# One level of Strassen in the second MoE product of a fused attention and MoE kernel

## The chip, the cores and the metric

The kernel runs on one core of a Trainium2 chip. The time is the device time of one execution in microseconds (us), as the median of several executions. The span in a profile is shorter than the time of the same execution (before: 435.7 and 437.55), so spans are compared only with spans. TensorE is called PE below (PEld is its loading of weights), VectorE DVE, ScalarE ACT and GpSimd POOL, as in the profile.

## The reference

Attention over 8 batches of 12 heads, 448 tokens and head size 64, with normalised q and k; its output goes through a two-layer MLP with a leaky ReLU. Cut to what matters:

```python
def _attn_ref(q, k, v, g_q, g_k):
    q_n, k_n = (rmsnorm(q, g_q), rmsnorm(k, g_k))
    scores = scale * np.matmul(q_n, k_n.transpose(0, 1, 3, 2))
    scores = scores - np.max(scores, axis=-1, keepdims=True)
    attn = np.exp(scores)
    attn = attn / (np.sum(attn, axis=-1, keepdims=True) + 1e-09)
    return np.matmul(attn, v)

def _moe_ref(x, w_in, w_out):          # x 3584 x 768, w_in 768 x 2048, w_out 2048 x 768
    h = x @ w_in
    g = np.maximum(0.01 * h, h)
    return g @ w_out
```

## The kernel before

Attention is worked in 24 units, three per batch. Each unit has four parts (d = 0 to 3). PE alternates between the scores of the unit and pieces of the MoE products, which come from a queue: `fill` takes pieces of it after each part, and weaves jobs for the other engines between them. The second product of the MoE takes tiles of 128 tokens; gt holds the activations of two batches, with the 2048 hidden features as 16 blocks on the partitions:

```python
    gt = cst.tile([P, FT, 2 * S], FP16)                 # FT = 16, S = 448
    ...
    def moe2(pair, t, half, part):                      # half: 384 of the 768 output columns
        ...
        for ft in range(8 * part, 8 * part + 8):
            nc.tensor.matmul(op2[:, 0:HC], gt[:, ft, ts(t, P)], wout16[:, ft, ds(HC * half, HC)],
                             start=(ft == 0), stop=(ft == FT - 1))
        if part == 0:
            return
        ...
            nc.vector.tensor_copy(ost[0][:, ds(HC * half, HC)], op2[:, 0:HC])
```

The exponentials of a new unit need a shift, which is made from the maximum of its first scores (DVE), spread over the partitions by a small matmul of `dg` (PE), and reduced again (DVE):

```python
                    qk(u, STEPS[d])                     # first scores of the new unit
                    if d == 0:
                        shift_max(u)                    # DVE: maximum of the scores, then dg
                        if narrow(u - 1):
                            pv_slot(u - 1)              # PE: 28 matmuls of the old unit
                            zcol(u - 1)                 # PE: 16 matmuls
                            shift_mm(u)                 # PE: the matmul of dg
                            ...
                    ex(u)                               # ACT: exponentials
```

On DVE the maximum stands behind whatever the last part of the old unit put there: the two normalisations `n` of a later unit, copies of finished output. On POOL run `xt` (x times 1/z), `rq` or `qg` (q times g) and some squares.

## Time and profile before

| | before |
|---|---|
| time, median (lowest to highest) | 436.96 us (436.82 to 437.01, 3 runs) |
| span of the profiled run | 435.7 us |
| busy: PE, DVE, ACT, POOL | 419.9, 215.6, 309.9, 148.8 us |
| mean granted clock of PE | 0.995 |

The row of PE's granted clock has one digit for each fortieth of the span, in tenths of full speed:

```profile
PEclk9899999999999999999999999999999999999999
```

After the second slice, which lies in the start, the digit never falls. The list of waits gives the waiting engine and line, the releaser, the total in us, the number and the longest:

```profile
PE sT L179 <- ACT et L198: 3.8, 9, 0.9
PE pb L228 <- DVE dg L218: 1.8, 3, 0.8
```

The second line is the matmul of dg; only one of its three waits, of 0.84 us, lies after the start. PE is all but free of waits.

### The profile page before, as it was taken

Reading aid. Unit: us, or ns where it says so; the run is one execution under the profiler, and the core shown is the slowest. Engines: PE = TensorE matmul, PEld = TensorE weight load, DVE = VectorE, ACT = ScalarE, POOL = GpSimd, SP = SyncE. Lnnn points to the kernel's source line nnn. Section 1 sums busy time; section 2 is a strip of 40 time slices with the busy share of each in tenths; the row PEclk is TensorE's granted clock in tenths of the full one; section 3 lists DMA queues with packets and bytes.
Section 4 is the critical chain, followed back from the end, with each engine's and each line's share of the span. In section 5 each row is a group of like instructions: output and inputs, shape, how many; then the busy total and the mean of one; then the engine's idle time right before and its main releaser. Section 6 shows DMA issues by size and latency. Waiting matters only on the chain.

```text
span 435.7 us, 8818 instructions
## 1 busy us (share of the span) xinstructions
PE 419.9 (96%) x3714; PEld 216.9 (50%) x3714; DVE 215.6 (49%) x321; ACT 309.9 (71%) x460; POOL 148.8 (34%) x102
## 2 busy tenths in 40 slices
PE   6878999999999999999999999999999999999995
PEld 6645444444455544554445544554445544555563
DVE  4897565874535744554455745555356611220021
ACT  5989878688976699867876699867877486634300
POOL 4997565633422432532430423522521110100000
PEclk9899999999999999999999999999999999999999
DMA  7999995789458856669447875778524530311022
GB/s 262 248 259 255 238 235 76 195 195 201 96 144 145 215 152 119 136 200 201 91 126 141 200 186 98 154 205 165 125 45 100 132 84 2 78 38 38 0 73 73
DMA packets 66315, 62.37 MB, mean 143 GB/s; under 512 B 35684, under 2 KB 61284, under 8 KB 66276
## 3 DMA queue, kind: packets, MB, share of 16 engines
q1 hardware_dynamic: 55840, 49.82, 44.7%
q0 software_dynamic: 10272, 11.80, 17.4%
q8 instruction: 29, 0.48, 0.4%
q10 hardware_dynamic: 164, 0.20, 0.1%
q14 instruction: 10, 0.08, 0.1%
HBM read 45.61 MB, written 11.01 MB: 130 GB/s over the span
## 4 chain that ended last, share of the span: by engine, by line
PE 84%; ACT 7%; DVE 6%; DMA 2%; issue 1%; SPq 0%; DVEq 0%; ACTq 0%
PE hps L329 33%; PE op L351 31%; PE sT L179 8%; PE sT L314 5%; ACT et L198 3%; PE zc L260 3%; DVE n L151 1%; DMA rk<-in_k_dram 1%; PE pb L228 1%; DVE ssq L139 1%; PE sT L243 1%; PE pv L314 1%; ACT et L196 1%; DVE xt L323 1%; DMA out_dram<-ost 1%
## 5 line engine op out<-in xcount | busy, mean ns | idle before, releaser
L198 ACT ACTIVATE et<-sT,eb 128x896 f16<-128x896 f32 x166 | 158.7, 1004 | 48.0 <-PE sT L179 35.7
L351 PE MATMUL op<-wout,gt 128*128 128x384 f16 x896 | 153.6, 326 | 0.0
L329 PE MATMUL hps<-xt,win 128*128 128x448 f16 x756 | 151.0, 353 | 0.2 <-DVE xt L323 0.2
L351 PEld LDWEIGHTS <-gt 128*128 128x128 f16 x896 | 84.7, 98 | 65.3 <-issue 12.2
L329 PEld LDWEIGHTS <-win 128*128 128x128 f16 x756 | 70.9, 98 | 71.8 <-issue 7.6
L294 POOL TENSOR_TENSOR xt<-x,rz 128x896 f16<-128x896 f32 x19 | 40.9, 2154 | 185.6 <-DMA rz<-zs 170.7
L331 ACT ACTIVATE gt<-hps 128x448 f16<-128x448 f32 x126 | 67.6, 543 | 22.6 <-PE hps L329 21.5
L359 DVE COPY ost<-op 128x384 f32<-128x384 f32 x54 | 30.0, 556 | 94.2 <-PE op L351 90.9
L134 POOL TENSOR_TENSOR qg<-rq,ggb 128x896 f32<-128x896 f32 (+2 forms) x25 | 61.3, 2454 | 36.9 <-DVE n L151 32.6
L179 PE MATMUL sT<-qkT 64*64 64x448 f16 x664 | 52.3, 364 | 4.5 <-ACT et L198 3.8
L151 DVE TENSOR_TENSOR n<-qg,rinv 128x896 f16<-128x896 f32 (+2 forms) x25 | 27.1, 1085 | 54.5 <-POOL xt L294 23.6
L139 DVE TENSOR_REDUCE ssq<-sq 128x14 f32<-128x896 f32 (+2 forms) x49 | 50.0, 1054 | 1.9 <-ACT sq L126 1.9
L216 DVE TENSOR_REDUCE sT<-sT 128x1 f32<-128x896 f32 x22 | 24.1, 1094 | 30.6 <-PE sT L179 30.4
L151 DVE TENSOR_TENSOR n<-rk,rinv 128x896 f16<-128x896 f32 (+2 forms) x25 | 34.2, 1372 | 0.0
L179 PEld LDWEIGHTS <-qkT 64*64 64x64 f16 x672 | 15.2, 104 | 37.9 <-issue 35.4
L272 ACT COPY x<-sT 128x896 f32<-128x896 f32 x19 | 17.2, 905 | 18.0 <-PE sT L314 18.0
L314 PE MATMUL sT<-et,vt 64*64 64x448 f16 x532 | 28.4, 349 | 0.0
L314 PEld LDWEIGHTS <-vt 64*64 64x64 f16 x672 | 19.8, 107 | 10.5
L106 POOL DMA_DIRECT2D vt<-in_v_dram x24 | 18.3, 763 | 0.0
L126 ACT ACTIVATE sq<-rq 128x896 f32<-128x896 f32 (+2 forms) x19 | 17.3, 913 | 1.2 <-DMA rq<-in_q_dram 1.2
L126 ACT ACTIVATE sq<-rk 128x896 f32<-128x896 f32 x17 | 16.2, 955 | 0.7 <-DMA rk<-in_k_dram 0.7
L260 PE MATMUL zc<-et,onesr 128*32 128x448 f16 (+1 forms) x304 | 16.1, 332 | 0.0
(66 smaller groups left out, 216.3 us busy)
## 6 DMA issues: line engine op xcount, KB each, us to landing
rq<-in_q_dram SPq DMA_DIRECT2D x24, 448.0 KB, 4.6
rk<-in_k_dram SPq DMA_DIRECT2D x24, 448.0 KB, 6.1
out_dram<-ost SPq DMA_DIRECT2D x54, 192.0 KB, 3.5
rz<-zs SPq DMA_DIRECT2D x38, 224.0 KB, 3.5
vt<-in_v_dram POOLq DMA_DIRECT2D x24, 224.0 KB, 4.7
win<-in_moe_w_in_dram POOLq DMA_DIRECT2D x8, 384.0 KB, 11.5
wout<-in_moe_w_out_dram POOLq DMA_DIRECT2D x2, 1536.0 KB, 26.9
qkT<-n SPq DMA_TRANSPOSE x18, 4.1
```

The lines of the kernel that those rows point to most:

```text
L126: nc.scalar.activation(buf(u, "sq")[:, ti, :, c[0]:c[1]], raw[u][ti][:, :, c[0]:c[1]], AF.Square)
L134: eng.tensor_tensor(buf(u, "qg")[:, :, c[0]:c[1]], raw[u][0][:, :, c[0]:c[1]], ggb[:, None, None, :].broadcast_to([P, 2, n, D]), op=ALU.mult)
L139: nc.vector.tensor_reduce(buf(u, "ssq")[:, ti, :, c[0]:c[1]], buf(u, "sq")[:, ti, :, c[0]:c[1]], axis=AXL.X, op=ALU.add)
L151: nc.vector.tensor_tensor(buf(u, "n16")[:, ti, c[0]:c[1]].rearrange("p s a d -> p a s d"), src[:, :, c[0]:c[1]], buf(u, "rinv")[:, ti, :, ...
L179: nc.tensor.matmul(banks[a][64 * r:64 * r + 64, 0:S].rearrange("p (t x) -> p t x", t=NS), kT(u, r, a, t), qT(u, r, a), start=True, stop=True)
L198: nc.scalar.activation(s["et"][:, t], sT[:, :, 0:S], AF.Exp, bias=s["eb"], scale=1.0)
L294: nc.gpsimd.tensor_tensor(xts[b][:, g], s["x32"], s["rz"], op=ALU.mult)
L314: nc.tensor.matmul(s["pv"][r][64 * a:64 * a + 64, 0:S], vts[u % NV][64 * r:64 * r + 64, a, t], s["et"][64 * r:64 * r + 64, t, a], start=(t ...
L329: nc.tensor.matmul(hps[:, 0:S], win16[:, kt // 2, kt % 2, ts(ft, P)], xt[:, kt // 2, kt % 2], start=(kt == 0), stop=(kt == KT - 1))
L331: nc.scalar.activation(gt[:, ft, ds(S * (b % 2), S)], hps[:, 0:S], AF.Prelu, bias=0.0, scale=1.0, alpha=0.01)
L351: nc.tensor.matmul(op2[:, 0:HC], gt[:, ft, ts(t, P)], wout16[:, ft, ds(HC * half, HC)], start=(ft == 0), stop=(ft == FT - 1))
L359: nc.vector.tensor_copy(ost[0][:, ds(HC * half, HC)], op2[:, 0:HC])
```

## The change

The intent is to take an eighth off the matmuls of each pair of token tiles in the second product; 11 pairs use it, which takes away 88 of the 896 matmuls. For two token tiles A = (a11 a12; a21 a22), split by halves of the hidden features, and the weights B split into four blocks, a product by blocks takes 8 half products of 8 matmuls each. Strassen's scheme, in the form with four sums on either side (s1 to s4 of the activations, four of the weights), takes 7. The sums of the weights are made once. Three of the seven half products are accumulated in PSUM onto others, and the rest is added on DVE on the way out. To make room in SBUF, gt shrinks to one batch and a carry of 64 columns, q times g is written in place, and some pools lose a buffer; the matmul of dg becomes two of 64 columns in spare columns of another bank. The core of the diff:

```diff
-    NV = 5
+    NV = 4
...
-    gt = cst.tile([P, FT, 2 * S], FP16)
+    gt = cst.tile([P, FT, 8 * 64], FP16)
+    tw = cst.tile([P, 4, HF, HC], FP16)          # sums of weights; HF = 8, HC = 384
+    sa = cst.tile([P, 4, HF, P], FP16)           # sums of activations
...
+        if u > 0 and "pslot" in st[u - 1]:       # in shift_mm: dg in two
+            pb = st[u - 1]["pslot"][:, :, S:S + 64]
+            for x in range(2):
+                nc.tensor.matmul(pb[:, x], onesp, s["dg"][:, 64 * x:64 * x + 64], start=True, stop=True)
...
+    def weight_sum(n, x):
+        x = slice(4 * x, 4 * x + 4)
+        a, b = ((wblock(0, 1), wblock(0, 0)), (wblock(1, 1), tw[:, 0]),
+                (wblock(1, 1), wblock(0, 1)), (wblock(1, 0), tw[:, 1]))[n]
+        nc.vector.tensor_tensor(tw[:, n, x], a[:, x], b[:, x], op=ALU.subtract)
+    def s1(tt, x=slice(0, 8)):
+        nc.vector.tensor_tensor(sa[:, 0, x], gblock(tt[1], 0)[:, x], gblock(tt[1], 1)[:, x], op=ALU.add)
+    def s2(tt, x=slice(0, 8)):
+        nc.vector.tensor_tensor(sa[:, 1, x], sa[:, 0, x], gblock(tt[0], 0)[:, x], op=ALU.subtract)
+    ...                                          # s3 = a11 - a21, s4 = a12 - s2, on nc.gpsimd
+    def seven(pair, tt, nxt=None, last=False):   # i0 to i6, each 8 matmuls; "later": at the next piece
+        i0: mm(bank("ma"), gblock(tt[0], 0), wblock(0, 0), True)    # later: DVE copies ma
+        i1: mm(bank("mb"), sa[:, 1], tw[:, 1], True)                # later: DVE adds mb
+        i2: mm(g["ma"], gblock(tt[0], 1), wblock(1, 0), False)      # later: ACT copies ma
+        i3: mm(bank("mc"), sa[:, 0], tw[:, 0], True)                # later: DVE adds mc, s1 of the next pair
+        i4: mm(bank("md"), sa[:, 2], tw[:, 2], True)                # later: DVE adds md
+        i5: mm(g["mc"], sa[:, 3], wblock(1, 1), False)              # later: s2, DVE adds mc, s3, s4
+        i6: mm(g["md"], gblock(tt[1], 1), tw[:, 3], False)          # later: DVE adds md
...
+                if d == 3 and u in (5, 6):
+                    for n in (0, 2) if u == 5 else (1, 3):
+                        for x in range(2):
+                            job(weight_sum, n, x)
```

(The lines i0 to i6 are shortened here from small functions to one line each.)

More of the change, by code (lines that the diff above doesn't have):

```diff
@@ L47 @@
     prep_p = ctx.enter_context(tc.tile_pool(name="prep", bufs=2))
-    small = ctx.enter_context(tc.tile_pool(name="small", bufs=3))
+    small = ctx.enter_context(tc.tile_pool(name="small", bufs=2))
     epool = ctx.enter_context(tc.tile_pool(name="epool", bufs=2))
-    zpool = ctx.enter_context(tc.tile_pool(name="zpool", bufs=2))
+    zpool = ctx.enter_context(tc.tile_pool(name="zpool", bufs=1))
     xpool = ctx.enter_context(tc.tile_pool(name="xpool", bufs=2))
-    opool = ctx.enter_context(tc.tile_pool(name="opool", bufs=3))
+    opool = ctx.enter_context(tc.tile_pool(name="opool", bufs=4))
     psum = ctx.enter_context(tc.tile_pool(name="psum", bufs=1, space=bass.MemoryType.PSUM))
@@ L77 @@
     wout16 = cst.tile([P, FT, DM], FP16)
-    gt = cst.tile([P, FT, 2 * S], FP16)
+    gt = cst.tile([P, FT, 8 * 64], FP16)
+    HF = FT // 2
+    HC = DM // 2
+    tw = cst.tile([P, 4, HF, HC], FP16)
+    sa = cst.tile([P, 4, HF, P], FP16)
     win_v = moe_w_in.rearrange("(g a r d) n -> a d g r n", a=2, r=2, d=D)
@@ L111 @@
     SHAPES = dict(
-        sq=([P, 2, 2, NS, D], FP32, 2), ssq=([P, 2, 2, NS], FP32, 2), uu=([P, 2, 2, NS], FP32, 2),
-        rinv=([P, 2, 2, NS], FP32, 2), qg=([P, 2, NS, D], FP32, 1),
-        n16=([P, 2, NS, 2, D], FP16, 2), qkT=([P, 2, NS, P], FP16, 3))
+        sq0=([P, 2, NS, D], FP32, 3), sq1=([P, 2, NS, D], FP32, 3), ssq=([P, 2, 2, NS], FP32, 2), uu=([P, 2, 2, NS], FP32, 2),
+        rinv=([P, 2, 2, NS], FP32, 2),
+        n16=([P, 2, NS, 2, D], FP16, 1), qkT=([P, 2, NS, P], FP16, 3))
     def buf(u, name):
@@ L118, in buf @@
             shape, dtype, bufs = SHAPES[name]
-            st[u][name] = prep_p.tile(shape, dtype, tag=name, bufs=bufs, name=name)
+            st[u][name] = prep_p.tile(shape, dtype, tag=name[:2] if bufs == 3 and name != "qkT" else name, bufs=bufs, name=name)
         return st[u][name]
@@ L125, in prep_sq @@
         for ti in tis:
-            nc.scalar.activation(buf(u, "sq")[:, ti, :, c[0]:c[1]], raw[u][ti][:, :, c[0]:c[1]], AF.Square)
+            nc.scalar.activation(buf(u, f"sq{ti}")[:, :, c[0]:c[1]], raw[u][ti][:, :, c[0]:c[1]], AF.Square)
     def prep_sqp(u, tis=BOTH):
         for ti in tis:
-            nc.gpsimd.tensor_tensor(buf(u, "sq")[:, ti], raw[u][ti], raw[u][ti], op=ALU.mult)
+            nc.gpsimd.tensor_tensor(buf(u, f"sq{ti}"), raw[u][ti], raw[u][ti], op=ALU.mult)
     def prep_qg(u, eng, c=ALL):
         n = c[1] - c[0]
-        eng.tensor_tensor(buf(u, "qg")[:, :, c[0]:c[1]], raw[u][0][:, :, c[0]:c[1]],
+        eng.tensor_tensor(raw[u][0][:, :, c[0]:c[1]], raw[u][0][:, :, c[0]:c[1]],
                           ggb[:, None, None, :].broadcast_to([P, 2, n, D]), op=ALU.mult)
@@ L138, in prep_ssq @@
         for ti in tis:
-            nc.vector.tensor_reduce(buf(u, "ssq")[:, ti, :, c[0]:c[1]], buf(u, "sq")[:, ti, :, c[0]:c[1]],
+            nc.vector.tensor_reduce(buf(u, "ssq")[:, ti, :, c[0]:c[1]], buf(u, f"sq{ti}")[:, :, c[0]:c[1]],
                                     axis=AXL.X, op=ALU.add)
@@ L149, in prep_norm @@
         for ti in tis:
-            src = (buf(u, "qg"), raw[u][1])[ti]
+            src = raw[u][ti]
             nc.vector.tensor_tensor(
@@ L224, in shift_mm @@
         s = st[u]
-        if "pb" not in s:
-            shift_bank(u)
-        pb = s["pb"]
-        nc.tensor.matmul(pb[:, 0:P], onesp, s["dg"], start=True, stop=True)
-        nc.vector.tensor_reduce(s["spare"][:, 510:511], pb[:, 0:P], axis=AXL.X, op=ALU.max)
+        if u > 0 and "pslot" in st[u - 1]:
+            pb = st[u - 1]["pslot"][:, :, S:S + 64]
+            for x in range(2):
+                nc.tensor.matmul(pb[:, x], onesp, s["dg"][:, 64 * x:64 * x + 64], start=True, stop=True)
+            nc.vector.tensor_reduce(s["spare"][:, 510:511], pb, axis=AXL.XY, op=ALU.max)
+        else:
+            if "pb" not in s:
+                shift_bank(u)
+            pb = s["pb"]
+            nc.tensor.matmul(pb[:, 0:P], onesp, s["dg"], start=True, stop=True)
+            nc.vector.tensor_reduce(s["spare"][:, 510:511], pb[:, 0:P], axis=AXL.X, op=ALU.max)
         s["eb"] = small.tile([P, 1], FP32, tag="eb", name="eb")
@@ L323, in xmul, with prelu @@
             nc.vector.tensor_tensor(xts[b][:, g, r], s["pv"][r][:, 0:S], s["rz"][:, r], op=ALU.mult)
+    def prelu(b, dst, src):
+        if b % 2 == 0:
+            src = src.rearrange("p (t x) -> p t x", t=NS)[:, ::-1]
+            dst = dst.rearrange("p (t x) -> p t x", t=NS)
+        nc.scalar.activation(dst, src, AF.Prelu, bias=0.0, scale=1.0, alpha=0.01)
     def moe1(b, ft):
@@ L330, in moe1 @@
                              start=(kt == 0), stop=(kt == KT - 1))
-        nc.scalar.activation(gt[:, ft, ds(S * (b % 2), S)], hps[:, 0:S], AF.Prelu,
-                             bias=0.0, scale=1.0, alpha=0.01)
+        prelu(b, gt[:, ft, 64 * (b % 2):64 * (b % 2) + S], hps[:, 0:S])
     def moe1_part(b, banks, k0, k1):
@@ L338, in moe1_part, with col, store, flush @@
                                  start=(kt == 0), stop=(kt == KT - 1))
-    ost = {}
+    def col(t):
+        return 64 * (5 - 2 * t) if t < 3 else P * (t - 3)
+    def store(pair, t, tile_, c, last):
+        for y in range(2):
+            n = 2 * t + (1 - y if t < 3 else y)
+            b, grp = 2 * pair + n // NS, n % NS
+            dst = out[b * S:(b + 1) * S, :].rearrange("(p t) m -> p t m", t=NS)
+            eng = nc.scalar if last and y else nc.sync
+            eng.dma_start(dst[:, grp, c], tile_[64 * y:64 * y + 64, c])
+    ost = {}
+    pend = []
+    L, R, LR = slice(0, HC), slice(HC, DM), slice(0, DM)
+    def flush():
+        while pend:
+            pend.pop(0)()
+    def out_tile():
+        return opool.tile([P, DM], FP32, tag="ost", name="ost")
     def moe2(pair, t, half, part):
-        last = pair == B // 2 - 1 and t == NS - 1
+        flush()
         if half == 0 and part == 0:
-            ost[0] = opool.tile([P, DM], FP32, tag="ost", name="ost")
+            ost[0] = out_tile()
         if part == 0:
@@ L348, in moe2 @@
         op2 = ost[1]
-        HC = DM // 2
         for ft in range(8 * part, 8 * part + 8):
-            nc.tensor.matmul(op2[:, 0:HC], gt[:, ft, ts(t, P)], wout16[:, ft, ds(HC * half, HC)],
+            nc.tensor.matmul(op2[:, 0:HC], gt[:, ft, ds(col(t), P)], wout16[:, ft, ds(HC * half, HC)],
                              start=(ft == 0), stop=(ft == FT - 1))
@@ L354, in moe2 @@
             return
-        if last:
-            nc.vector.tensor_copy(ost[0][:, HC * half:HC * half + HC // 2], op2[:, 0:HC // 2])
-            nc.scalar.copy(ost[0][:, HC * half + HC // 2:HC * half + HC], op2[:, HC // 2:HC])
-        else:
-            nc.vector.tensor_copy(ost[0][:, ds(HC * half, HC)], op2[:, 0:HC])
-        if half == 1 or last:
-            c = slice(HC * half, HC * half + HC) if last else slice(0, DM)
-            for y in range(2):
-                bb, grp = divmod(2 * t + y, NS)
-                b = 2 * pair + bb
-                dst = out[b * S:(b + 1) * S, :].rearrange("(p t) m -> p t m", t=NS)
-                eng = nc.scalar if last and y else nc.sync
-                eng.dma_start(dst[:, grp, c], ost[0][64 * y:64 * y + 64, c])
@@ L369 @@
-    queue = []
-    def push_moe1(b):
-        for ft in range(FT):
-            queue.append((1.13, lambda b=b, ft=ft: moe1(b, ft)))
-    def push_moe2(b):
-        for t in (range(3) if b % 2 == 0 else range(3, 7)):
-            for half in range(2):
-                for part in range(2):
-                    queue.append((1.31, lambda b=b, t=t, half=half, part=part: moe2(b // 2, t, half, part)))
+        nc.vector.tensor_copy(ost[0][:, ds(HC * half, HC)], op2[:, 0:HC])
+        if half == 1:
+            store(pair, t, ost[0], LR, False)
@@ new lines, in wblock, with gblock @@
+    def wblock(i, j):
+        return wout16[:, HF * i:HF * i + HF, HC * j:HC * j + HC]
+    def weight_sum(n, x):
[3 more added lines that the diff above has]
+        nc.vector.tensor_tensor(tw[:, n, x], a[:, x], b[:, x], op=ALU.subtract)
+    def gblock(t, j):
+        return gt[:, HF * j:HF * j + HF, ds(col(t), P)]
+    def s1(tt, x=slice(0, 8)):
+        nc.vector.tensor_tensor(sa[:, 0, x], gblock(tt[1], 0)[:, x], gblock(tt[1], 1)[:, x], op=ALU.add)
@@ new lines, in s2, with s3, s4, later @@
+    def s2(tt, x=slice(0, 8)):
+        nc.vector.tensor_tensor(sa[:, 1, x], sa[:, 0, x], gblock(tt[0], 0)[:, x], op=ALU.subtract)
+    def s3(tt, x=slice(0, 8)):
+        nc.gpsimd.tensor_tensor(sa[:, 2, x], gblock(tt[0], 0)[:, x], gblock(tt[1], 0)[:, x], op=ALU.subtract)
+    def s4(tt, x=slice(0, 8)):
+        nc.gpsimd.tensor_tensor(sa[:, 3, x], gblock(tt[0], 1)[:, x], sa[:, 1, x], op=ALU.subtract)
+    def later(fn, *args):
+        pend.append(lambda: fn(*args))
+    def seven(pair, tt, nxt=None, last=False):
+        g = {}
+        def mm(bank, a, b, first):
+            for f in range(HF):
+                nc.tensor.matmul(bank[:, 0:HC], a[:, f], b[:, f], start=(first and f == 0), stop=(f == HF - 1), skip_group_check=not first)
+        def bank(name):
+            g[name] = aux([P, 512], FP32, name)
+            return g[name]
+        def add(dst, src, name):
+            nc.vector.tensor_tensor(dst, g[name][:, 0:HC], src, op=ALU.add)
+        def put(i, c):
+            store(pair, tt[i], g["o"][i], c, last)
+        def i0():
+            flush()
+            g["o"] = (out_tile(), out_tile())
+            mm(bank("ma"), gblock(tt[0], 0), wblock(0, 0), True)
+            later(lambda: nc.vector.tensor_copy(g["o"][1][:, L], g["ma"][:, 0:HC]))
+        def i1():
+            flush()
+            mm(bank("mb"), sa[:, 1], tw[:, 1], True)
+            later(lambda: add(g["o"][1][:, L], g["o"][1][:, L], "mb"))
+        def i2():
+            flush()
+            mm(g["ma"], gblock(tt[0], 1), wblock(1, 0), False)
+            later(lambda: nc.scalar.copy(g["o"][0][:, L], g["ma"][:, 0:HC]))
+            if last:
+                later(put, 0, L)
+        def i3():
+            flush()
+            mm(bank("mc"), sa[:, 0], tw[:, 0], True)
+            later(lambda: add(g["o"][1][:, R], g["o"][1][:, L], "mc"))
+            if nxt:
+                later(s1, nxt)
+        def i4():
+            flush()
+            mm(bank("md"), sa[:, 2], tw[:, 2], True)
+            later(lambda: add(g["o"][1][:, R], g["o"][1][:, R], "md"))
+            if last:
+                later(put, 1, R)
+        def i5():
+            flush()
+            mm(g["mc"], sa[:, 3], wblock(1, 1), False)
+            if nxt:
+                later(s2, nxt)
+            later(lambda: add(g["o"][0][:, R], g["o"][1][:, L], "mc"))
+            later(put, 0, R if last else LR)
+            if nxt:
+                later(s3, nxt)
+                later(s4, nxt)
+        def i6():
+            flush()
+            mm(g["md"], gblock(tt[1], 1), tw[:, 3], False)
+            later(lambda: add(g["o"][1][:, L], g["o"][1][:, L], "md"))
+            later(put, 1, L if last else LR)
+        return [i0, i1, i2, i3, i4, i5, i6]
@@ new lines, with also, both, push @@
+    queue = []
+    def also(fn, *more):
+        def both():
+            fn()
+            for m in more:
+                m()
+        return both
+    def push(b):
+        pair, odd = divmod(b, 2)
+        fast = b > 0
+        order = [f // 2 + HF * (f % 2) for f in range(FT)] if odd else range(FT)
+        items = [(1.13, lambda ft=ft: (flush(), moe1(b, ft))) for ft in order]
+        half = [(slice(0, 4)), (slice(4, 8))]
+        if odd:
+            tt, tn = (3, 4), (5, 6)
+            for n, x in ((8, 0), (FT - 1, 1)):
+                c, fn = items[n]
+                items[n] = (c, also(fn, *[lambda f=f, x=x: later(f, tt, half[x]) for f in (s1, s2, s3, s4)]))
+            items += [(1.31, fn) for fn in seven(pair, tt, tn)]
+            items += [(1.31, fn) for fn in seven(pair, tn, None, b == B - 1)]
+        else:
+            tiles = (2,) if fast else (0, 1, 2)
+            std = [lambda t=t, h=h, p=p: moe2(pair, t, h, p) for t in tiles for h in range(2) for p in range(2)]
+            if fast:
+                tt = (0, 1)
+                std[0] = also(std[0], lambda: later(s1, tt))
+                std[1] = also(std[1], lambda: later(s2, tt))
+                std[2] = also(std[2], lambda: later(s3, tt), lambda: later(s4, tt))
+                std += seven(pair, tt)
+            items += [(1.31, fn) for fn in std]
+        queue.extend(items)
@@ L410, in fill @@
             job()
+        flush()
     vcopy, acopy = nc.vector.tensor_copy, nc.scalar.copy
@@ L585 @@
         xmul(2)
-        push_moe1(0)
-        push_moe2(0)
+        push(0)
         first = slot()
@@ L593 @@
         moe1_part(0, first, KT - 1, KT)
-        nc.scalar.activation(gt[:, 0:2, 0:S], first[:, :, 0:S], AF.Prelu, bias=0.0, scale=1.0, alpha=0.01)
+        for ft in range(2):
+            prelu(0, gt[:, ft, 0:S], first[:, ft, 0:S])
         del queue[0:2]
@@ L638 @@
                 if fed(u, d) and u > 3:
-                    push_moe1(u // NQ - 1)
-                    push_moe2(u // NQ - 1)
+                    push(u // NQ - 1)
                 if (u, d) in ((3, 1), (4, 0)):
@@ L661 @@
         xmul(NU - 1)
-        push_moe1(B - 1)
-        push_moe2(B - 1)
+        push(B - 1)
         while queue:
             queue.pop(0)[1]()
+        flush()
 _INS = ['q', 'k', 'v', 'g_q', 'g_k', 'moe_w_in', 'moe_w_out']
```

## The prediction

> **What bounds the kernel now.** I read the page first: the busy shares, then the chain that ended last. The chain is almost all TensorE:
>
> ```profile
> span 435.7 us, 8818 instructions
> PE 419.9 (96%) x3714; PEld 216.9 (50%) x3714; DVE 215.6 (49%) x321; ACT 309.9 (71%) x460; POOL 148.8 (34%) x102
> ...
> PE 84%; ACT 7%; DVE 6%; DMA 2%; issue 1%; SPq 0%; DVEq 0%; ACTq 0%
> ```
>
> A busy PE need not be a full PE, so I next read the chain in order of time near the end:
>
> ```profile
> 392.39 18.16 PE hps L329 x96
> 410.55 18.21 PE op L351 x112
> ```
>
> The second product (op, line 351) takes 18.21 us for 112 matmuls of 384 columns, 162.6 ns each; the first (hps) 18.16 for 96 of 448 columns, 189 ns. They follow each other without a gap, and the stretches of 50 us from 100 to 350 us each show PE busy for 50.00. So from about 60 us on the end is set by the number of columns that PE must stream. A matmul removed there is worth its 162.6 ns, provided that nothing new makes PE wait.
>
> How near the other engines are to making it wait decides this case, so I then read the timelines of DVE, POOL and PE at the seam between two units of attention (a unit is a third of a batch). PE does the first scores of the new unit, then pv (28 matmuls) and zc (16), then one matmul of dg, which DVE must have made by then: a maximum of the scores, then dg. At a usual seam:
>
> ```profile
> 295.29 1.09 DVE L216 TENSOR_REDUCE sT<-sT 128x1 f32<-128x896 f32 x1
> 296.41 0.29 DVE L218 TENSOR_TENSOR dg<-ident,sT 128x128 f16<-128x128 f16 x1
> ...
> 296.34 0.85 PE L260 MATMUL zc<-et,onesr 128*32 128x448 f16 x16
> 297.12 0.23 PE L228 MATMUL pb<-dg,onesp 128*128 128x128 f16 x1
> ```
>
> dg is ready at 296.70, PE wants it at 297.12: DVE has 0.4 us to spare. At the seam near 85 us it has none:
>
> ```profile
> 81.53 2.98 DVE L151 TENSOR_TENSOR n<-rk,rinv 128x896 f16<-128x896 f32 x1
> 84.43 0.55 DVE L359 COPY ost<-op 128x384 f32<-128x384 f32 x1
> 84.90 1.08 DVE L216 TENSOR_REDUCE sT<-sT 128x1 f32<-128x896 f32 x1
> ...
> 80.82 2.73 POOL L294 TENSOR_TENSOR xt<-x,rz 128x896 f16<-128x896 f32 x1 [3.95 <-DMA rz<-zs]
> 83.52 2.93 POOL L134 TENSOR_TENSOR qg<-rq,ggb 128x896 f32<-128x896 f32 x1
> ...
> 86.35 0.22 PE L228 MATMUL pb<-dg,onesp 128*128 128x128 f16 x1 [0.84 <-DVE dg L218]
> ```
>
> The reader is to see that n, 1.08 us long elsewhere, took 2.98, and ended 0.96 us after POOL's xt did: it lay blocked until xt was done. POOL's qg in turn took 2.93 where others take 2.08: it waited for n. The maximum came late, and PE stood for 0.84 us.
>
> **What the Trainium skill says.** "SBUF — State Buffer", section "Who interferes with whom": a DVE instruction with two SBUF inputs contends with a GpSimd instruction that reads SBUF, and the one that comes second blocks for the whole of the other. The lines above agree. "VectorE: DVE Perf Modes", section "The perf-mode tier table": an add of two 16-bit SBUF tensors takes two elements a cycle, 1224 ns for 2048 elements; no such add with enough elements is in this trace, so I use it as an estimate: 1024 cycles at 0.96 GHz are 1067 ns, leaving 157 fixed. "TensorE: Matmul & The Clock Gate", section "Wait — 56ns, not 53.3ns?": start to start is N/2.4 GHz plus about 2.5 ns, 162.5 ns for 384 columns; the trace has 162.6. The same page, "What's actually happening": an idle window of about 3.4 us lets the clock fall to half. No stretch after the start of this trace idles PE so long.
>
> **The change part by part.**
> 1. Removed on PE: a pair of token tiles costs 7 x 8 matmuls instead of 8 x 8. Batches 1, 3, 5, 7 do two such pairs, batches 2, 4, 6 one; batch 0 none. 11 pairs by 8 are 88 of the 896 matmuls; by 162.6 ns, **-14.3 us**, all on the bounding engine.
> 2. The dg matmul becomes two of 64 columns, in spare columns of the pv bank, at 19 seams. A seam costs 0.16 us now; two loads of weights for less streaming may add 0.05: **+0.9 us**. Also, the built program makes ACT's copy of that bank (x) wait for DVE's maximum of pb, so ACT starts its exponentials some 0.7 us later per unit; ACT has idle gaps of 1 us and more in most units, so I count nothing beyond a few tenths.
> 3. Sums of weights, once: 8 additions of 1536 fp16 elements, each 768/0.96 + 157 = 957 ns (some 0.88 start to start). The built order places four of them on DVE after n and directly before the maximum at the seam near 85 us, the other four likewise at the next, near 99 us. DVE's slack there is -0.84 and +0.3. Four cost 3.5 us, so 3.5 + 3.2 = 6.7 us of new PE wait is the floor. They have two SBUF inputs, and qg stands waiting on POOL just there: it goes first, for 2.07 us, of which 2.1 and 1.5 us could come on top: 10.3. I take **+8.8 us**.
> 4. Merges, per pair: six PSUM operations on DVE (a copy and five additions) in place of four copies of 556 ns, and one copy on ACT. s1 and s2 are 690 ns each on DVE (1024/2/0.96 + 157). By kind: 56 copies go (-30.7 us); 12 + 11 copies (12.8), 55 additions at about 550 ns (30.3), s1 and s2 (16.5), weights (7.7) come: +36.6, DVE at some 252 us. On POOL, s3 and s4 at 2.31 ns an element (xt: 2.07 us for 896) are 2.4 us each, 11 pairs: +52, to some 201. Both stay far below PE, and most of it lies beside other work.
> 5. But the seams have only 0.4 us. In a unit with Strassen work, DVE has n twice, s1 or s2, the addition of the last product and the maximum to do, with xt, s3, s4 and qg on POOL in between. Laying these out by hand from the rows' durations, I get seams without a wait when POOL is out of the way, and up to 3 us late when n or s1 loses to two POOL operations. About twelve seams are concerned; at 0.35 us on average, **+4.2 us**.
> 6. In odd batches the second product needs s2, which needs the last Prelu: 0.58 + 2 x 0.42 us against 1.3 us of the first product; POOL's s3 (1.2 us) may come in between. In the middle the scores cover some of it, in batch 7 nothing does: **+1.4 us** over four batches.
> 7. Removed buffers (vts, zpool, small, n16, in-place q*g): each new wait is for something that ends a good part of a unit earlier; nothing. The end after the last matmul is as before: an eviction and a write of 96 KB.
>
> Sum: -14.3 + 0.9 + 8.8 + 4.2 + 1.4 = +1.0; since the two stalls of part 3 let the others catch up once, I round this down to nothing: **437 us**.
>
> **The rivals.**
> (a) The saving arrives whole: PE is the bound, DVE and POOL have room on average, and the change is carefully laid out (postponed merges, sums in halves, reordered first product). Then 437 - 14.3 + 0.9 + some tenths = 424. For it: the 96% and the chain. Against it: the 0.4 us at the seams and the four additions before the maximum, which are in the built order.
> (b) Only the weight sums hurt, at their floor, and the clock stays up: 437 - 14.3 + 0.9 + 6.7 + 1 = 431.
> (c) DVE and POOL block each other at each Strassen seam, by 1.2 us at twelve: 10 us more than I count, 447; and if the two stalls of 4 to 6 us drop PE's clock for a window, 1 to 2 us each on top: 450.
> (d) ACT becomes the bound in the first product: its exponentials start later. ACT is busy 58.84 of 72 us in the stretch from 240 to 312; PE's work per unit shrinks but the first product is spread thinner by the same pacing. I give this little.
>
> **Range and chances.** Faster than 428.2 (2%) needs all new waits under 6.5 us, below the floor of part 3 alone; only a DVE order that proves harmless gives it: 0.14. Slower than 445.7 needs (c): 0.12. Within: 0.74. Range 428 to 446.
>
> **What would show it.** PE's busy time falls by about 14 us while the span hardly moves. The waits list shows PE held by DVE's dg, with two of 3.5 to 6 us where the unit seams near 85 and 99 us are, right after four additions of line 400; some more, up to 3 us, at seams with Strassen work, next to lengthened n, s1 or s2 on DVE; in the tail one wait of 0.3 to 1.6 us before the second product of batch 7. Matmuls of 384 columns number 808, still near 163 ns. I am wrong if the waits on dg at the two weight seams are small, if PE waits for ACT instead, or if the weight sums run at half the rate I take (then 6 us slower).

## The result, and the profile after

The changed kernel takes 443.72 us (441.66 to 445.02, 4 runs), the kernel before 436.99 beside it. The ratio is 1.0145, with a 95% interval of 1.0103 to 1.0188. Ratios are the mean time of one kernel's fast runs over that of the other's of the same rounds, so they are not quite the ratios of the medians. So the change costs 1.5%: within 2%, but the product with a tenth fewer matmuls (808 of 896) made the kernel slower. The mean granted clock of its four executions was 0.976 to 0.988; the fastest, 441.66 us, had the highest.

The page of the changed kernel:

```profile
span 443.2 us, 8892 instructions
...
PE 413.9 (93%) x3645; PEld 211.8 (48%) x3645; DVE 256.6 (58%) x381; ACT 309.6 (70%) x470; POOL 191.5 (43%) x132
...
PEclk9699999969699999999999999999999999999999
...
PE 69%; DVE 12%; ACT 11%; issue 5%; DMA 2%; SPq 0%; DVEq 0%; ACTq 0%
```

PE's busy time fell by only 6.0 us, not by 14; its share of the chain fell from 84% to 69%, and that of DVE doubled. The clock row shows two slices at 6 (from 88.6 and from 110.8 us) where the kernel before has 9; the 6 in the second slice lies in the start, where the clock stood at half for 6.8 us (12.36 to 19.18 us), against 3.4 us in the kernel before. The list of waits:

```profile
PE sT L232 <- DVE dg L222: 12.7, 5, 6.1
PE sT L183 <- ACT et L202: 3.8, 9, 0.9
PE md L425 <- DVE ost L432: 1.5, 4, 0.4
```

The waits on ACT at line 183 are what they were. The waits on dg are new: five, of 6.07, 3.78, 2.16, 0.53 and 0.20 us. The third line is new too: four times 0.37 us, in which the second half product into md waits until DVE has added the first. The timelines of DVE, POOL and PE at the first of the five (columns: start, duration, engine, line, operation, count, and in brackets the idle time before it with what ended it):

```profile
82.51 2.97 DVE L155 TENSOR_TENSOR n<-rk,rinv 128x896 f16<-128x896 f32 x1
85.41 2.83 DVE L400 TENSOR_TENSOR tw<-wout 128x1536 f16<-128x1536 f16 x1
88.16 0.54 DVE L389 COPY ost<-op 128x384 f32<-128x384 f32 x1
88.63 2.68 DVE L400 TENSOR_TENSOR tw<-wout 128x1536 f16<-128x1536 f16 x3
91.23 1.08 DVE L220 TENSOR_REDUCE sT<-sT 128x1 f32<-128x896 f32 x1
...
84.50 2.93 POOL L138 TENSOR_TENSOR rq<-rq,ggb 128x896 f32<-128x896 f32 x1
...
92.69 0.26 PE L232 MATMUL sT<-dg,onesp 128*128 128x64 f16 x2 [6.07 <-DVE dg L222]
92.77 5.18 PE L385 MATMUL op<-wout,gt 128*128 128x384 f16 x16
```

Four weight sums stand before the maximum (line 220). Three of them took 2.68 us together; the first one alone took 2.83, because POOL's rq held it up to 87.43. PE waited 6.07 us, and then sixteen matmuls took 5.18 us that take 2.76 at other seams. The second weight seam is alike:

```profile
105.78 5.43 DVE L400 TENSOR_TENSOR tw<-wout,tw 128x1536 f16<-128x1536 f16 x4
...
112.60 0.27 PE L232 MATMUL sT<-dg,onesp 128*128 128x64 f16 x2 [3.78 <-DVE dg L222]
112.68 6.27 PE L345 MATMUL hps<-xt,win 128*128 128x448 f16 x18
```

Eighteen of these matmuls take 3.57 us at full clock, as an experiment below shows at the same place. The account of the profiled runs, in us:

| item | worked out as | us |
|---|---|---|
| matmuls removed | 88 x 0.1626 | -14.3 |
| waits on dg | 12.74 less 0.84 of before | +11.9 |
| waits on md | 4 x 0.37 | +1.5 |
| slow clock after the two long waits | (5.18 - 2.76) + (6.27 - 3.57) | +5.1 |
| start, up to the first matmul of dg in two | 73.89 - 72.95 | +0.9 |
| sum | | +5.1 |
| spans | 443.2 - 435.7 | +7.5 |

About 2.4 us stay. Most of them lie in how the list counts, from the modelled end of the last matmul; the starts of the matmuls show more. Each wait on md is 0.37 us in the list, but the matmul behind it starts 0.70 us after the one before it instead of 0.16, which makes 0.6 us more for the four; the waits on dg come to 12.4 us over before instead of 11.9; at three seams pv waits for ACT's exponentials, 0.27 us each by the starts; and one wait on ma costs 0.3. Together these are 2.2 to 2.3 us.

### The profile page after: what moved, and what is told of

The parts are those of the page before. It is cut to its first block, busy times and chain, and to the rows that moved or that the text cites.

```text
span 443.2 us, 8892 instructions
## 1 busy us (share of the span) xinstructions
PE 413.9 (93%) x3645; PEld 211.8 (48%) x3645; DVE 256.6 (58%) x381; ACT 309.6 (70%) x470; POOL 191.5 (43%) x132
## 4 chain that ended last, share of the span: by engine, by line
PE 69%; DVE 12%; ACT 11%; issue 5%; DMA 2%; SPq 0%; DVEq 0%; ACTq 0%
PE hps L345 31%; ACT et L202 7%; PE sT L183 6%; PE ma L425 6%; PE md L425 5%; PE op L385 5%; PE sT L324 4%; PE mc L425 3%; PE mb L425 3%; DVE n L155 3%; PE zc L270 2%; DVE tw L400 2%; DVE sT L220 2%; DMA rq<-in_q_dram 2%; DVE ost L432 1%
## 5 line engine op out<-in xcount | busy, mean ns | idle before, releaser
L138 POOL TENSOR_TENSOR rq<-rq,ggb 128x896 f32<-128x896 f32 (+2 forms) x25 | 52.4, 2097 | 41.8 <-ACT sq L130 28.6
L155 DVE TENSOR_TENSOR n<-rq,rinv 128x896 f16<-128x896 f32 (+2 forms) x25 | 31.4, 1259 | 60.0 <-issue 42.4
L425 PEld LDWEIGHTS <-sa 128*128 128x128 f16 x352 | 32.8, 98 | 26.3 <-issue 6.1
L412 POOL TENSOR_TENSOR sa<-gt 128x512 f16<-128x512 f16 (+1 forms) x15 | 25.8, 1722 | 28.4 <-ACT gt L339 24.5
L385 PE MATMUL op<-wout,gt 128*128 128x384 f16 x192 | 36.5, 342 | 0.0
L425 PEld LDWEIGHTS <-gt 128*128 128x128 f16 x264 | 25.2, 98 | 20.6 <-issue 4.6
L415 POOL TENSOR_TENSOR sa<-gt,sa 128x512 f16<-128x512 f16 (+1 forms) x15 | 26.7, 1778 | 15.1 <-DVE sa L409 10.5
L425 PE MATMUL ma<-wout,gt 128*128 128x384 f16 x176 | 32.3, 326 | 0.1
L155 DVE TENSOR_TENSOR n<-rk,rinv 128x896 f16<-128x896 f32 (+2 forms) x25 | 29.9, 1197 | 0.0
L406 DVE TENSOR_TENSOR sa<-gt 128x512 f16<-128x512 f16 (+1 forms) x15 | 10.6, 708 | 30.3 <-ACT gt L339 30.3
L385 PEld LDWEIGHTS <-gt 128*128 128x128 f16 x192 | 18.4, 102 | 15.5 <-issue 5.7
```

The lines of the kernel that those rows point to most:

```text
L138: eng.tensor_tensor(raw[u][0][:, :, c[0]:c[1]], raw[u][0][:, :, c[0]:c[1]], ggb[:, None, None, :].broadcast_to([P, 2, n, D]), op=ALU.mult)
L155: nc.vector.tensor_tensor(buf(u, "n16")[:, ti, c[0]:c[1]].rearrange("p s a d -> p a s d"), src[:, :, c[0]:c[1]], buf(u, "rinv")[:, ti, :, ...
L385: nc.tensor.matmul(op2[:, 0:HC], gt[:, ft, ds(col(t), P)], wout16[:, ft, ds(HC * half, HC)], start=(ft == 0), stop=(ft == FT - 1))
L425: nc.tensor.matmul(bank[:, 0:HC], a[:, f], b[:, f], start=(first and f == 0), stop=(f == HF - 1), skip_group_check=not first)
```

## The experiments

Theory A, formed from these lines, says that a seam costs what stands before its maximum on DVE, lengthened by POOL where both want SBUF, plus a loss of clock after a long wait. The rivals are that Strassen's additional vector work costs time wherever it stands, and that the smaller buffers and the other parts of the change cost it. Each e-number below is an edit of the changed kernel. Runs e1 to e4 shared one chip and the same runs of before (437.0 us), e5 to e7 another set (437.19).

### e1_sums_later: the weight sums after the maximum

```diff
-                if d == 3 and u in (5, 6):
-                    for n in (0, 2) if u == 5 else (1, 3):
+                if d == 0 and u in (7, 8):
+                    for n in (0, 2) if u == 7 else (1, 3):
```

> The changed kernel, but the eight weight sums stand right after the softmax-sum work of units 7 and 8, where DVE idles for some 7 us, instead of directly before the maximum of the seams into units 6 and 7. Theory A (the sums before the seam cost 9.0 us of PE waits, 6.07 + 3.78 less 0.84, and the clock drop that follows costs 5.1 us more): both waits on dg fall under 1 us, no half-clock stretch after 60 us, 443.7 - 14.1 = 429.6 us, ratio about 0.983. Rival B (the Strassen merges and the DVE/POOL lock cost it, the sums' waits would only be paid elsewhere): 437 or more. Rival C (only the waits go, the slow matmuls have another cause): 434.7.

Measured: 429.6 us (429.21 to 431.39, 4 runs), ratio 0.9836 (0.9812 to 0.986). It is 14.1 us faster than the changed kernel with the same instructions, and 1.6% faster than the kernel before. The two long waits are gone. So no cost of making the sums shows; what they cost came from their place.

This run shows one thing more. Both kernels have a wait of 2.16 us at the seam into the same unit, first the changed kernel, then e1 (timeline of PE):

```profile
149.88 0.22 PE L232 MATMUL sT<-dg,onesp 128*128 128x64 f16 x2 [2.16 <-DVE dg L222]
149.94 1.46 PE L425 MATMUL mc<-wout,sa 128*128 128x384 f16 x8
151.24 1.46 PE L425 MATMUL md<-tw,gt 128*128 128x384 f16 x8
```

```profile
134.99 0.25 PE L232 MATMUL sT<-dg,onesp 128*128 128x64 f16 x2 [2.16 <-DVE dg L222]
135.05 2.75 PE L425 MATMUL mc<-wout,sa 128*128 128x384 f16 x8
137.59 1.90 PE L425 MATMUL md<-tw,gt 128*128 128x384 f16 x8
```

The same wait left the clock up in one execution and cost 1.73 us in the other (2.75 + 1.90 - 2 x 1.46). The Trainium skill ("TensorE: Matmul & The Clock Gate", section "What's actually happening") calls the window in which PE's activity is judged free-running; that one wait has two outcomes agrees with it. The traces show what decided. Within each trace the changes of the granted clock lie whole multiples of 3.41 us apart (changed kernel: 90.86, 97.69, 111.34 and 118.17 us). Continued to the waits, these steps of 3.41 us divide them so (idle time of PE is the step less PE's busy time in it):

| run, wait on dg | step of 3.41 us | PE idle in it | clock after it |
|---|---|---|---|
| changed, 3.78 us | 107.93 to 111.34 | 2.52 us | half |
| changed, 2.16 us | 145.48 to 148.89, and the next | 1.17 and 0.99 us | full |
| e1, 2.16 us | 131.64 to 135.05 | 2.16 us | half |
| e3, 2.58 us | 191.18 to 194.59 | 2.59 us | half |
| e7, 1.90 us | 106.43 to 109.84 | 1.90 us | full |

After 60 us every full-clock step of the nine traces with 2.16 us of idle time or more was followed by half clock, and none with 1.90 or less. So in these runs a wait of 2.16 us cost when it fell whole into one step, and not when it lay across two; where the steps lie differs from execution to execution. The granted clocks of e1's four executions are 0.991 twice and 0.999 twice, so the loss probably fell in two of them. In the start, steps with 1.6 to 1.9 us of idle time were followed by half clock as well, so idle time alone is not the whole rule, and no run tests it further.

### e2_half_later: only the second four sums moved

```diff
-                if d == 3 and u in (5, 6):
+                if (u, d) in ((5, 3), (8, 0)):
```

> Only the second four sums are moved (to unit 8); the first four stay before the seam into unit 6. Theory A: the wait of 6.1 us at the first seam and its slow matmuls (2.5 us) stay, those of the second (3.8 + 2.7) go: 443.7 - 6.5 = 437.2 us. Rival B: about 443. If the wait moved on instead of going, a new wait on dg of some 4 us shows at a later seam.

Measured: 436.87 us (436.66 to 436.97, 4 runs), ratio 0.9994 (0.9979 to 1.0009). The longest wait on dg is still 6.1 us, the one of 3.78 is gone. The two weight seams are worth about 7 us each (443.72 to 436.87 to 429.6), and they add up.

### e3_keep_warm: small matmuls in the long waits

100 and 60 matmuls of 128 columns, whose results nobody reads, stand before the matmul of dg at the two weight seams, so that PE is not idle there:

```diff
                             zcol(u - 1)
+                            if u in (6, 7):
+                                warm(100 if u == 6 else 60, aux([P, 512], FP32, "warm"))
                             shift_mm(u)
```

> The changed kernel with 100 and 60 idle matmuls of 128 columns (some 5.6 and 3.4 us of PE work, into a spare PSUM bank, read by nobody) put before the dg matmul of the seams into units 6 and 7, where PE stands waiting. Theory A: they fill the waits without lengthening them, PE does not go to half clock, and the 5.1 us of slow matmuls go: 438.6 us, with 16 op matmuls after the first seam at 2.7 us instead of 5.2. Rival C (the slow matmuls are not from the clock falling in the wait): unchanged, 443.7, or longer by what the dummies overshoot.

Measured: 441.75 us (439.44, 440.05, 443.45 and 443.86), ratio 1.0105 (1.0056 to 1.0154). The first half of the expectation held:

```profile
85.50 5.76 PE L561 MATMUL warm<-onesp 128*128 128x128 f16 x100
91.64 0.22 PE L232 MATMUL sT<-dg,onesp 128*128 128x64 f16 x2 [0.38 <-DVE dg L222]
91.69 2.76 PE L385 MATMUL op<-wout,gt 128*128 128x384 f16 x16
```

The sixteen matmuls take 2.76 us again, and the eighteen at the second seam 3.57. So the slow stretches came from PE's idleness, and their 5.1 us are real. But the gain did not arrive whole. In the profiled run (443.86) the units now fall differently in time, and two other things went wrong: the second pause grew from 3.78 to 5.0 us (3.52 of small matmuls and 1.48 of wait), as n was held up by POOL's xt just before; and a seam that never waited before got a wait of 2.58 us, where s2 (2.48 us in place of 0.68) lay behind rq on POOL. After it the clock fell:

```profile
194.25 0.22 PE L232 MATMUL sT<-dg,onesp 128*128 128x64 f16 x2 [2.58 <-DVE dg L222]
194.30 4.44 PE L385 MATMUL op<-wout,gt 128*128 128x384 f16 x16
```

That wait and its clock loss (4.44 - 2.76) are 4.3 us, and the four times lie in two groups some 4 us apart. It is likely that only two of the four executions had it: their granted clocks are 0.994 in both long ones, 0.996 and 0.999 in the short ones. But only one was profiled.

### e4_plain_product: everything but Strassen

The old order of products with the new buffers, q times g in place, gt of one batch and a carry, and dg in two:

```diff
-                if d == 3 and u in (5, 6): ...            (the weight sums)
-        fast = b > 0
+        fast = False
-        if odd: ... seven(pair, tt, tn) ...
+        if odd: items = moe1(b, ft) for all ft, then moe2(pair, t, h, p) for tiles 3 to 6
```

> The changed kernel with the plain second product for every tile and no weight sums: what is left is the smaller buffers, the in-place product of q and g, the carry layout of gt, the two-part dg matmul in the pv bank. Theory A: they cost next to nothing, 437 to 438.5 us (the changed kernel's start was 0.9 us longer in the profile, its clock rising later). Rival D (the smaller buffers and the later x copy cost several us and hide part of the gain): 440 or more.

Measured: 438.74 us (438.44 to 438.92, 4 runs), ratio 1.0039 (1.0022 to 1.0055). The profiles show where: every unit from the first of the 19 seams with dg in two to the last has the length that it has before, within 0.25 us (296.98 us in all against 296.63), and PE ends its last matmul at 431.34 us against 431.35. What is longer is the end after it, by 0.7 us, probably because this edit also loses the special split of the last tile's eviction that the kernel before has. The other 1 us between the medians is not located: the profiled execution of before is one of its longer ones (437.55 us) and ran 3.4 us of its start at half clock, which that of e4 did not, so it may lie in the start. So the buffers and dg in two cost some 1 us by the medians, and are not where the rest of the time went.

### e5_operands_after_max: e1, with s1 to s4 after the maximum too

Sums of activations that fall due in the last part of a unit wait in a second list until the shift is out, or until a product needs them:

```diff
     def later(fn, *args):
-        pend.append(lambda: fn(*args))
+        (lazy if fn in (s1, s2, s3, s4) else pend).append(lambda: fn(*args))
 ...                                   # in flush(), after pend: "if not hold[0]: release()"; release() empties lazy
             flush()                   # in i1
+            release()
             mm(bank("mb"), sa[:, 1], tw[:, 1], True)
 ...                                   # at the seam, after shift_mm, pv_out and zcol_sum
+                        hold[0] = False
+                        release()
 ...
+                hold[0] = d == 3
                 fill(u, d, jobs)
```

> Edit: e1_sums_later, and in addition every operand addition (s1 to s4) that falls due in the last part of a unit is held back until the shift of the next unit's exponentials is out, so that none stands before a maximum on VectorE. Theory A (what stands before the maximum on VectorE is what a seam costs): the waits of 2.16, 0.17 and 0.16 us before the dg matmul that e1 still shows go away, and with the first of them the clock loss of 1.67 us that e1's profiled run shows after it; 429.6 less 2.5 gives 427.1, with a narrower spread (e1: 429.2 to 431.4), and the list of waits has no seam of a Strassen unit. Rival B (the seam wait only moves: the operands now come too late for the second product): a wait of about as much before mb appears, 429 to 430. Rival C (the late additions delay VectorE's sums of zs and with it the next xt): waits of PE on xt or et, over 430.

Measured: 427.32 us (426.57 to 427.97, 4 runs), ratio 0.9768 (0.9751 to 0.9785), against 427.1 from theory A. The wait of 2.16 us became 0.22 (timeline of PE):

```profile
132.98 0.22 PE L232 MATMUL sT<-dg,onesp 128*128 128x64 f16 x2 [0.22 <-DVE dg L222]
```

This came with the same two lengthened n before the maximum; it was s1, moved from between them and the maximum, that made the rest. No wait before mb appeared.

### e6_second_norm_later: e5, with one normalisation moved

```diff
                     if d == 2:
                         job(prep_rinv, u + 2)
-                        for ti in range(2):
-                            job(prep_norm, u + 2, ALL, (ti,))
-                        if u > 3:
-                            job(prep_trd, u + 2)
+                        job(prep_norm, u + 2, ALL, (0,))
+                        if u <= 3:
+                            job(prep_norm, u + 2, ALL, (1,))
+                    if d == 3 and u > 3:
+                        job(prep_norm, u + 2, ALL, (1,))
+                        job(prep_trd, u + 2)
```

> Edit: e5, and the second normalisation (rk) and the transposing load behind it moved from the third part of a unit to its last part, so that the addition of md stands before it on VectorE. Theory A: the four waits of 0.37 us of PE on the addition of md (1.5 us in all) go, the rest stays: 427.1 less 1.5 gives 425.6. Rival B (the normalisation, 1.1 us and up to 3 us when POOL works beside it, now stands right before the maximum and uses up the slack there): waits before the dg matmul return in several units, 427 to 432.

Measured: 425.96 us (425.53 to 427.49, 5 runs), ratio 0.9746 (0.9727 to 0.9765), against 425.6. The waits on md are gone from the list, and small waits on dg came in their place: two of 0.27 us, at seams that e5 passes without one. In the same rounds e5's median is 1.4 us longer, but the two intervals overlap: that the waits are gone is shown, the gain in time from this one step is likely. This is the fastest version, 2.5% under the kernel before.

### e7_unlock: the sums in place, POOL out of their way

```diff
-                    if u + 2 < NU:
+                    if u + 2 < NU and u not in (6, 7):
                         prep_qg(u + 2, nc.gpsimd)
 ...
+                    if u == 5:
+                        prep_qg(8, nc.gpsimd)       # before xt of unit 4 instead of after it
                 if d == 1 and u > 3 and narrow(u - 1):
                     xmul_pool(u - 1)
+                    if u == 7:
+                        prep_qg(9, nc.gpsimd)       # after xt of unit 6
```

> Edit: the changed kernel with its weight sums where they are, but the two POOL multiplications by g that ran beside the weight sums (2.93 us at 84.5 us and 2.50 us at 107.9 us) moved away: one in front of the product x*rz before it, one behind the product of the next unit. Theory A (a vector sum that wants to start while POOL multiplies stands still until POOL is done, so a part of the two long waits is POOL's): the four sums before each of the two seams take about 3.5 us start to end instead of 5.2 and 5.4; the waits fall from 6.07 and 3.78 to about 4.2 and 1.9, the second clock loss of 2.7 us goes, and 443.7 becomes about 437. Rival B (the sums are this slow by themselves, the overlap with POOL is chance): waits and time stay, 443 to 444. Rival C (POOL's multiplication moved meets other vector work instead): the waits shrink by less than 1 us and the time stays over 441.

Measured: 439.28 us (439.03 to 439.77, 4 runs), ratio 1.0043 (1.0028 to 1.0058). The weight sums and the two waits, from the timelines of DVE and PE:

```profile
84.83 0.95 DVE L400 TENSOR_TENSOR tw<-wout 128x1536 f16<-128x1536 f16 x1
86.16 2.68 DVE L400 TENSOR_TENSOR tw<-wout 128x1536 f16<-128x1536 f16 x3
103.66 3.56 DVE L400 TENSOR_TENSOR tw<-wout,tw 128x1536 f16<-128x1536 f16 x4
...
90.23 0.27 PE L232 MATMUL sT<-dg,onesp 128*128 128x64 f16 x2 [4.65 <-DVE dg L222]
108.59 0.22 PE L232 MATMUL sT<-dg,onesp 128*128 128x64 f16 x2 [1.90 <-DVE dg L222]
```

The first sum fell from 2.83 to 0.95 us, the four of the second seam from 5.43 to 3.56. So 1.9 us of each long wait was POOL's, as the Trainium skill has it ("SBUF — State Buffer", section "Who interferes with whom"): the vector instruction with two SBUF inputs stood still until POOL's was done. After the wait of 1.90 the eighteen matmuls take 3.57 us: no clock loss. After the one of 4.65 the sixteen take 5.31 us, so that loss stayed. The expected 437 was missed by 2.3 us, because the moved rq did harm elsewhere: at the first seam the first n grew from 1.08 to 1.54 us (hence 4.65 in place of 4.2); and before the third seam n had to wait until the late rq ended at 120.99, then lay behind POOL's s3 (2.03 us), which made a wait of 1.81 us that the changed kernel does not have.

## Why the prediction was right or wrong

The predicted 437.0 with 428 to 446 held the measured 443.7, and within 2% was the right class, near its edge. That owes something to luck: the sum of no change was 6.7 us too low, with costs counted that did not occur and larger ones left out. By its own steps:

1. The removed matmuls: right. 808 matmuls of 384 columns are left. With the long waits out of the way e1 gets 7.4 us of the 14.3, e6 11.2.
2. dg in two, +0.9: wrong, it costs nothing that shows. In e4 the two matmuls take 0.23 us and the next one starts 0.07 us after the first, as before with one.
3. The weight sums, +8.8: right in mechanism and in size. 6.07 - 0.84 + 3.78 are 9.0; an undisturbed sum took 944 ns where 957 was estimated, and e7 shows the share of the lock, 1.9 us at each seam. e1 and e2 show that the place is the cost, with nothing left over that shows.
4. The load of DVE and POOL: 256.6 and 191.5 us against 252 and 201. POOL's s3 and s4 took 2.13 us, not 2.4.
5. The other seams, +4.2: right in sum by luck, 2.16 + 0.53 + 0.20 on dg and 1.5 on md are 4.4. The spread was not as pictured: instead of a little at twelve seams, one seam carries half of it, and the waits on md were not foreseen. e5 and e6 took both away, each by about what the waits showed.
6. The wait for s2 in odd batches, +1.4: wrong, it does not occur. In batch 7, timelines of DVE and PE:

```profile
422.04 0.42 DVE L409 TENSOR_TENSOR sa<-sa,gt 128x512 f16<-128x512 f16 x1
...
420.80 1.46 PE L425 MATMUL ma<-wout,gt 128*128 128x384 f16 x8
422.10 1.46 PE L425 MATMUL mb<-tw,sa 128*128 128x384 f16 x8
```

   mb starts while the second half of s2 is still running, without a gap after ma. Its first four matmuls read only the first half of s2; the working waited for the whole.
7. The buffers, nothing: right as far as e4 can tell, with about 1 us open.

The step that failed is the one that was left out of the sum. "If the two stalls of 4 to 6 us drop PE's clock" stood in rival (c), at 1 to 2 us each; the sum itself rounded down, because the stalls should let others catch up. The stalls came at the predicted length and the clock did fall: 2.4 and 2.7 us, 5.1 together, which e3 shows by taking them away with matmuls whose results nobody reads. With parts 2 and 6 struck out (-2.3), this term (+5.1), the start (+0.9), the small waits (+2.4) and the 1.0 that was rounded away make nearly the whole difference. One sum beside it is wrong too: 428.2 leaves room for 5.5 us of new waits (428.2 - 422.7), not 6.5; both lie below the floor of 6.7, so the conclusion stands. Having quoted the skill's idle window of 3.4 us and predicted two waits above it, the prediction should have counted the loss in the sum.

Rival (a), the saving whole at 424, was wrong for this order of instructions, but e6 comes within 2 us of it, so the bound was read rightly: the columns on PE set the end, and what took the gain was a few instructions before a maximum. Rival (d), ACT, did not occur: PE's waits on ACT at the scores are 3.8 us in both kernels, and the new ones of pv come to 0.8.

## What to carry to other kernels

When an extra piece of work goes to an engine that is half idle, ask what stands behind it in that engine's order, not how busy the engine is: four additions, 3.6 us together, cost about 7 us before a maximum, with the lock and the loss of clock that came with them, and nothing that shows behind it. Where the bounding PE pauses for 2 us or more, allow for a loss of clock behind the pause (here 1.7 to 2.7 us, or none), and look for the lock between DVE and POOL wherever a vector instruction takes two or three times its usual length. Moving such an instruction also moves the collisions of others, so each edit has to be read again seam by seam.

## What the Trainium skill lacked or had wrong

- "TensorE: Matmul & The Clock Gate", section "HAM oscillation — how this bites in real kernels", gives the rule that PE should have no idle gaps over about 3.4 us. Here waits of 2.16 us (e1) and 2.58 us (e3) already cost 1.7 us each; the same wait of 2.16 us in the changed kernel, and 1.90 in e7, cost nothing. After 60 us the clock fell where one step of 3.41 us held 2.16 us or more of idle time, so a gap well under 3.4 us can already cost.
- "GPSIMD Engine Reference", section "3.1 Elementwise — side-by-side cycle accounting", measures a two-input addition in fp32 alone. Here 1024 fp16 elements take 2.13 us, 2.08 ns each, so the rate in fp16 is close to the page's fp32 figure (4497 ns for 2048).
